# Attention plus gated MLP: later rows regrouped through DRAM and turned by VectorE, last stores split in two

## The chip, the cores and the metric

The kernel runs on one core of a Trainium2 chip. The metric is the device time of one execution in microseconds. Names used below: PE or TensorE (matmuls; its weight loads are PEld), DVE or VectorE, ACT or ScalarE, POOL or GpSimd, and SP, the engine whose queue issues most DMAs. SBUF is the on-chip memory, PSUM holds the matmul results in eight banks, DRAM is the off-chip memory.

## The reference

One layer over 2048 rows of 640 values: a layer norm, then the sum of the input, a sliding-window attention (32 heads of 20, window 256) and a gated MLP (width 1536).

```python
xn = _layernorm(x)                               # x: (1, 2048, 640), bfloat16
# A: attention
qkv = (xn @ wqkv) -> q, k, v                     # 32 heads, Dh = 20
scores = einsum("bhqd,bhkd->bhqk", q, k) * Dh ** -0.5
mask = (i - j >= 0) & (i - j < 256)
A = softmax(where(mask, scores, -1e9)) @ v -> (1, 2048, 640) @ wo
# B: gated MLP
B = (sigmoid(xn @ w_gate) * (xn @ w_up)) @ w_down
return x + A + B
```

## The kernel before

The 2048 rows are four chunks of 512 (`c`), each of four row blocks of 128 (`s`). All matmuls contract over the partitions, so the normalized rows must stand with the 640 columns on the partitions: `xnT[c]` is 128 x 5 x 512, where plane `d` holds 128 of the 640 columns. Every weight that is multiplied with it (`wqkv`, `wg`, `wu`) lies as 128 x 5 x n with the same assignment of columns to partition and plane. Before the change, partition p of plane d is column d * 128 + p.

How `xnT` comes about differs by chunk. Chunk 0 is turned by TensorE (`transpose_rows`, L276: five identity matmuls for a row block, then a copy from PSUM). Chunks 1 to 3 go through `g_norms` (L343): statistics of the four row blocks, a few steps of pause, then `norm_block` writes a normalized block `xn`, and `turn_block` (L283) has SP issue a DMA transpose of it into `xnT[c]`; for chunk 3 the transposes are issued by a generator of their own, `g_turns`.

A hand-written order runs everything. The attention scores (`scores`, L487 matmuls, L493 exponential on ScalarE, masks on GpSimd at L504) come in 76 steps; after each, the class `Fill` issues as much of the other work as fits a credit. That other work is a list of parts: "gu0a" and "gu0b" (gate and up projections of chunk 0, in halves of 5 matmuls; `pg` at L411, `pu` at L418, and the product `h` on VectorE at L422), then "x2" (load of chunk 2's rows), "wo_i" (eight DRAM-to-DRAM copies that rearrange `wo`, L212), "wd" (five loads, L205), "pads" (two clears of scratch, L178), "qk1" (q and k projections of chunk 1), "v1", "out0" (down projection, `y` at L432 and L439, and the output rows), "x3", "qk2" and so on. `mix` lets the steps of `g_norms` slip in between: after every step of "gu0b" one step of chunk 1's, after every step of "out0" one of chunk 2's, and chunk 3's in "gu1b" and in every second step of "out1". Each engine's instructions, and each queue's DMAs, run in the order in which they are issued.

What the steps below touch:

- The input rows of a chunk lie in the tile `xc`, of which there is one buffer (`pool("xp", 1)`). A new load into it (L140) waits until the last reader of the old rows is done.
- A projection (`proj_block`, L297) fills a PSUM bank, VectorE (q) or ScalarE (k) casts it into a tile `st` (L301, L303), and SP stores that to a DRAM scratch (L305). There are six `st` buffers. `spread` (L315) loads q and k back with heads on partitions.
- The PSUM pool `ps_d` has four banks and serves `pqk`, `pv`, `pg`, `pu`, `y` and the attention sum `acc` (L520) in turn; `ps`, the scores, has one buffer of four banks.
- `finish_group` and `scale_group` run on VectorE after each `acc` (L532 to L548), and `add_x` (L443) adds the input rows to `y`.
- The last row block of chunk 3 is finished in three column pieces (0 to 320, 320 to 512, 512 to 640), each stored by one DMA, on ACT's, SP's and ACT's queue.

Of the kernel before, what the change touches and what calls it, by code (L numbers as in the profile page):

```python
# [9 lines left out]
P = 128  # L10
S = 2048
D = 640
# [3 lines left out]
DC = D // P  # L16
FC = F // P
CW = 512
NCH = S // CW
SBC = CW // P  # L20
# [6 lines left out]
FS = 768  # L27
# [10 lines left out]
BF16 = mybir.dt.bfloat16  # L38
# [7 lines left out]
U = 64  # L46
# [47 lines left out]
def kernel(  # L94
# [11 lines left out]
    nc = tc.nc  # L106
    x2 = A_x.flatten_outer_dims()
    out2 = out.flatten_outer_dims()
# [26 lines left out]
    xc = {}  # L135
# [4 lines left out]
        nc.sync.dma_start(out=t, in_=xr[:, c * SBC:(c + 1) * SBC, :])  # L140

    wqkv = [const.tile([P, DC, D], BF16, name="w" + part) for part in "qkv"]
    wqkv_r = A_wqkv.rearrange("(c p) n -> p c n", p=P)
    wg = [const.tile([P, DC, FS], BF16, name=f"wg{k}") for k in range(F // FS)]
    wu = [const.tile([P, DC, FS], BF16, name=f"wu{k}") for k in range(F // FS)]
    wd = const.tile([P, FC, D], BF16, name="wd")
# [32 lines left out]

    def load_gu(t, w, k, lo=0, hi=FS):  # L180
        nc.sync.dma_start(out=t[k][:, :, lo:hi],
                          in_=w.rearrange("(c p) f -> p c f", p=P)[:, :, k * FS + lo:k * FS + hi])

    load_gu(wg, B_w_gate, 0, 0, FS // 2)
    load_gu(wu, B_w_up, 0, 0, FS // 2)
    clear("q", 0)
    clear("k", 0)
# [33 lines left out]
    ident = const.tile([P, P], BF16, name="ident")  # L221
# [24 lines left out]
    xnT = {}  # L246
    xns = {}
# [13 lines left out]
    def ln_block(c, s, mv=None):  # L261
        return ln_mv(ln_half(c, s, 1, ln_half(c, s, 0)), mv)

    def rstd_blocks(mvs):
        rstds = lnp.tile([P, SBC], FP32, name="rstds", bufs=1)
        nc.gpsimd.tensor_scalar(out=rstds, in0=mvs[:, :, 1], scalar1=EPS, scalar2=None, op0=ADD)
        nc.gpsimd.tensor_tensor(out=rstds, in0=rstds, in1=neghalf, op=POW)
        return rstds

    def norm_block(c, s, mv, rstd):  # L270
        xn = lnp.tile([P, D], BF16, name="xn")
        nc.vector.tensor_scalar(out=xn, in0=xc[c][:, s, :], scalar1=mv[:, 0:1],  # L272
                                scalar2=rstd[:, 0:1], op0=SUB, op1=MULT)
        xns[c, s] = xn

    def transpose_rows(s, copy, lo=0, hi=DC):  # L276
        pt = ps_h.tile([P, DC, P], BF16, name="pt", tag="h")
        for d in range(lo, hi):
            nc.tensor.transpose(pt[:, d, :], xns[0, s][:, d * P:(d + 1) * P], ident)  # L279
        copy(out=xnT[0][:, lo:hi, s * P:(s + 1) * P], in_=pt[:, lo:hi, :])  # L280

    def turn_block(c, s):
        nc.sync.dma_start(out=xnT[c][:, :, s * P:(s + 1) * P], in_=xns.pop((c, s)), transpose=True)  # L283

    def new_xnT(c):
        xnT[c] = xtp.tile([P, DC, CW], BF16, name="xnT")
# [53 lines left out]

    MM = 216

    def g_norms(c, turn, gap=3):  # L343


        new_xnT(c)
        mvs = lnp.tile([P, SBC, nc.vector.BN_AGGR_DIM], FP32, name="mvs", bufs=1)
        for s in range(SBC):
            ln_block(c, s, mvs[:, s, :])
            if s == SBC - 1:  # L350
                rstds = rstd_blocks(mvs)
            yield 0
        for _ in range(gap):
            yield 0
        for s in range(SBC):
            norm_block(c, s, mvs[:, s, :], rstds[:, s:s + 1])
            yield 0
            if turn:
                turn_block(c, s)

    def g_turns(c):
        for s in range(SBC):
            turn_block(c, s)
            yield 0

    def g_qk(c):
        for w in "qk":
            for m in range(DC):
                proj_block(w, c, m)
                if c == 0 and w == "q" and m == 1:  # L370
                    load_x(1)
                if c == 0 and w == "q" and m == 3:
                    load_gu(wu, B_w_up, 0, FS // 2)
                if c == 1 and w == "q" and m == 3:
                    load_wo()
# [27 lines left out]
    def part(w, d, f):  # L403
        k, first = divmod(f * P, FS)
        return w[k][:, d, first:first + P]

    def g_gu(c, f0, f1):
        for f in range(f0, f1):
            pg = ps_d.tile([P, CW], FP32, name="pg", tag="d")
            for d in range(DC):  # L410
                nc.tensor.matmul(pg, lhsT=part(wg, d, f), rhs=xnT[c][:, d, :],  # L411
                                 start=(d == 0), stop=(d == DC - 1))
            th = tp.tile([P, CW], FP32, name="th")
            nc.scalar.activation(out=th, in_=pg, func=TANH, scale=0.5)  # L414
            yield 5 * MM
            pu = ps_d.tile([P, CW], FP32, name="pu", tag="d")
            for d in range(DC):
                nc.tensor.matmul(pu, lhsT=part(wu, d, f), rhs=xnT[c][:, d, :],  # L418
                                 start=(d == 0), stop=(d == DC - 1))
            h = hp.tile([P, CW], BF16, name="h")  # L420
            ht[c, f] = h
            nc.vector.scalar_tensor_tensor(out=h, in0=th, scalar=1.0, in1=pu, op0=ADD, op1=MULT)  # L422
            yield 5 * MM
# [6 lines left out]
    def down(c, s, y, cut):  # L430
        for f in range(FC):
            nc.tensor.matmul(y[:, 0:cut[1] - cut[0]], lhsT=ht[c, f][:, s * P:(s + 1) * P],  # L432
                             rhs=wd[:, f, cut[0]:cut[1]], start=(f == 0), stop=False)
            if f % 6 == 5:
                yield 6 * 136
# [11 lines left out]
    def new_rows(c, s, name="rows", bufs=3, queue=nc.sync):  # L447
        rows = lnp.tile([P, D], BF16, name=name, bufs=bufs)
        queue.dma_start(out=rows, in_=xr[:, c * SBC + s, :])
        return rows  # L450

    def store(c, s, rows, cut=(0, D), queue=nc.sync):
        sb = c * SBC + s
        queue.dma_start(out=out2[sb * P:(sb + 1) * P, cut[0]:cut[1]], in_=rows[:, cut[0]:cut[1]])

    def outp(c, s, ys, rows):
        for y, cut in zip(ys, HALVES):
            add_wo(c, s, y, cut)
        for y, cut in zip(ys, HALVES):
            add_x(y, cut, rows)  # L460
        store(c, s, rows)

    def g_out(c, between, ahead=()):
        nxt = new_rows(c, 0)
        for s in range(SBC):
            rows = nxt
# [128 lines left out]
    def mix(a, b, first, every=1, rest=True):  # L595

        for k, cost in enumerate(a):
            yield cost
            if k >= first and (k - first) % every == 0:
                yield next(b, 0)  # L600
        if rest:
            yield from b
# [74 lines left out]
    fill = Fill()  # L677
    GU = 10 * MM
    OUT = 4 * 34 * 136
    APART = 1800  # L680
    FIRST_PART = 1000
    def later(load, *args):
        load(*args)
        yield 0

    norms1 = g_norms(1, True)
    norms2 = g_norms(2, True)
    norms3 = g_norms(3, False, 6)
    fill.add("gu0a", mix(g_gu(0, 0, 4), norms1, 4, 1, False), 4 * GU)
    fill.add("gu0b", mix(g_gu(0, 4, 12), norms1, 0), 8 * GU)  # L690
    fill.add("x2", later(load_x, 2), 0)
# [7 lines left out]
    fill.add("qk2", g_qk(2), 50 * MM)  # L699
    fill.add("v2", mix(g_v(2), g_gu(1, 3, 7), 0, 1), 40 * 136 + 4 * GU)  # L700
    fill.add("gu1b", mix(g_gu(1, 7, 12), norms3, 0, 1, False), 5 * GU)
    fill.add("out1", mix(g_out(1, g_gu(2, 0, 1)), itertools.chain(norms3, g_turns(3)), 1, 2), OUT + GU)
    fill.add("qk3", g_qk(3), 50 * MM)
    fill.add("v3", mix(g_v(3), g_gu(2, 1, 5), 0, 1), 40 * 136 + 4 * GU)
    fill.add("gu2", g_gu(2, 5, 12), 7 * GU)
# [8 lines left out]
    cuts = [(ends[n, NG - 2] + 2 + n, f"out{n}") for n in range(NCH - 1)] + [(len(todo), None)]  # L714
# [4 lines left out]
    for t, (c, k, o, step) in enumerate(todo):  # L719
# [11 lines left out]
        pt, late = scores(c, o, step)  # L731
        parts.setdefault((c, o), []).append((step, pt))
        last, label = next(x for x in cuts if t < x[0])
# [10 lines left out]
    c = NCH - 1  # L744
# [6 lines left out]
    rows = [new_rows(c, s, *home, queue=nc.scalar) for s, home in enumerate(homes)]  # L751
# [8 lines left out]
    last = SBC - 1  # L760
    cuts = (HALVES[0], (HALF, 4 * P), (4 * P, D))
# [8 lines left out]
    add_down(last, cuts[1], ps_d, "d")  # L770
    for s in range(1, last):
        outp(c, s, [ys[s, cut] for cut in HALVES], rows[s])
    for cut, queue in zip(cuts, (nc.scalar, nc.sync, nc.scalar)):
        if cut == cuts[2]:
            add_down(last, cut, ps_y, "y")
        add_wo(c, last, ys[last, cut], cut)
        add_x(ys[last, cut], cut, rows[last])
        store(c, last, rows[last], cut, queue)
# [1 line left out]
_INS = ['A_x', 'A_wqkv', 'A_wo', 'B_x', 'B_w_gate', 'B_w_up', 'B_w_down']  # L780
_OUTS = [((1, 2048, 640), 'bfloat16')]
# [25 lines left out]
```

## Time and profile before

Three runs took 308.99, 309.4 and 310.95 us; the median is 309.4 us. One execution was profiled; its page gives the span from the first to the last instruction, and what lies around it is not on the page.

| | |
|---|---|
| median of 3 runs | 309.4 us |
| span of the profiled execution | 307.5 us |
| TensorE busy | 299.6 us |
| VectorE busy | 170.7 us |
| ScalarE busy | 198.4 us |
| GpSimd busy | 169.3 us |
| DMA: SP's queue (q1), share of 16 engines | 37.3% |
| granted TensorE clock, mean | 1.000 |

The lines shown in the prediction are of three kinds. A line of the page's first part gives an engine's busy time, its share of the span and its instructions. A line of the timeline gives start, duration (both in us), engine, source line, operation, output and input tiles, and how many instructions are merged in it; a bracket at its end tells what the engine waited for. A line of a tile's answer gives shortest, median and longest duration in ns and when the first and the last started.

### The profile page before, as it was taken

What the parts mean: (1) busy time and instruction counts of PE and PEld (TensorE: products, weight loads), DVE (VectorE), ACT (ScalarE), POOL (GpSimd) and SP (SyncE); (2) the same over time, 40 slices, a digit from 0 to 9 for tenths busy, and PEclk for the clock granted to TensorE, in tenths of its full rate; (3) what the DMA queues carried; (4) which work ended last, traced back from release to release, by engine and by line L of the source; (5) the groups of instructions that cost most, each with busy time, mean ns of one, the idle gap of its engine ahead of it and who ended that gap; (6) DMA issues with size and microseconds to landing.
All of it is one profiled execution on the core that took longest, in us unless ns stands there. A gap on an engine that the chain in (4) does not pass through costs nothing.

```text
span 307.5 us, 9944 instructions
## 1 busy us (share of the span) xinstructions
PE 299.6 (97%) x4276; PEld 167.5 (54%) x4311; DVE 170.7 (56%) x339; ACT 198.4 (65%) x197; POOL 169.3 (55%) x308
## 2 busy tenths in 40 slices
PE   7999999999999999999999999999999999999995
PEld 3654444555657654554457654554546664444774
DVE  5633666639698364487946164392824536363523
ACT  6933877698855649888674547878585547687000
POOL 6000686787874828576683729467372937566000
PEclk9999999999999999999999999999999999999999
DMA  7997976986407352820002712730000200000202
GB/s 215 366 344 236 324 158 214 337 238 209 154 2 139 58 179 68 272 83 2 3 3 67 129 58 87 250 122 0 5 0 2 87 26 21 2 2 7 83 21 67
DMA packets 40460, 35.68 MB, mean 116 GB/s; under 512 B 10560, under 2 KB 39872, under 8 KB 40384
## 3 DMA queue, kind: packets, MB, share of 16 engines
q1 hardware_dynamic: 39552, 34.27, 37.3%
q10 hardware_dynamic: 864, 0.77, 0.9%
q8 instruction: 34, 0.56, 0.8%
q14 instruction: 10, 0.08, 0.1%
HBM read 23.63 MB, written 10.26 MB: 110 GB/s over the span
## 4 chain that ended last, share of the span: by engine, by line
PE 96%; issue 1%; DMA 1%; DVE 1%; ACT 0%; SPq 0%
PE y L432 18%; PE pu L418 17%; PE pg L411 17%; PE pqk L297 14%; PE ps L487 9%; PE pv L326 7%; PE y L439 7%; PE acc L520 6%; DMA xc<-in_A_x_dram 1%; PE pt L279 0%; ACT xn L617 0%; DVE xn L272 0%; DVE xn L628 0%; SPq L156 0%; DVE stats L252 0%
## 5 line engine op out<-in xcount | busy, mean ns | idle before, releaser
L504 POOL TENSOR_SCALAR_AFFINE_SELECT pT<-pT 64x512 bf16<-64x512 bf16 (+1 forms) x256 | 157.7, 616 | 108.1 <-ACT pT L493 95.6
L493 ACT ACTIVATE pT<-ps 128x2048 bf16<-128x2048 f32 (+1 forms) x76 | 141.0, 1855 | 59.6 <-PE ps L487 54.6
L422 DVE SCALAR_TENSOR_TENSOR h<-th,pu 128x512 bf16<-128x512 f32 x48 | 32.8, 684 | 52.6 <-PE pu L418 46.1
L418 PE MATMUL pu<-xnT,wu 128*128 128x512 bf16 x228 | 59.0, 380 | 0.7 <-issue 0.2
L411 PE MATMUL pg<-xnT,wg 128*128 128x512 bf16 x226 | 58.5, 380 | 0.9 <-issue 0.3
L432 PE MATMUL y<-wd,h 128*128 128x320 bf16 (+2 forms) x396 | 56.7, 295 | 0.0
L432 PEld LDWEIGHTS <-h 128*128 128x128 bf16 x396 | 36.7, 98 | 15.8 <-issue 2.0
L414 ACT ACTIVATE th<-pg 128x512 f32<-128x512 f32 x48 | 28.6, 595 | 15.5 <-PE pg L411 15.4
L411 PEld LDWEIGHTS <-wg 128*128 128x128 bf16 x240 | 22.2, 98 | 25.8 <-issue 1.8
L418 PEld LDWEIGHTS <-wu 128*128 128x128 bf16 x240 | 22.0, 98 | 25.5 <-issue 2.0
L487 PE MATMUL ps<-qT,kT 20*64 20x320 bf16 (+4 forms) x1440 | 32.1, 260 | 0.0
L532 DVE STREAM_TRANSPOSE t<-acc 128x512 f32<-128x512 f32 x32 | 21.1, 697 | 19.7 <-PE acc L520 19.7
L487 PEld LDWEIGHTS <-kT 20*64 20x64 bf16 x1440 | 15.4, 103 | 24.9 <-issue 21.8
L443 DVE SCALAR_TENSOR_TENSOR rows<-y,rows 128x320 bf16<-128x320 f32 x30 | 14.4, 488 | 25.5 <-PE y L439 25.3
L544 DVE TENSOR_TENSOR on<-t,rec 128x320 bf16<-128x320 f32 (+4 forms) x48 | 27.8, 580 | 1.1
L326 PE MATMUL pv<-wv,xnT 128*128 128x320 bf16 x160 | 25.7, 300 | 0.0
L439 PE MATMUL y<-wo,oc 128*128 128x320 bf16 (+2 forms) x165 | 24.2, 295 | 0.0
L297 PE MATMUL pqk<-xnT,wk 128*128 128x512 bf16 x97 | 23.1, 381 | 0.2
L297 PE MATMUL pqk<-xnT,wq 128*128 128x512 bf16 x94 | 22.8, 381 | 0.4 <-issue 0.2
L335 DVE CAST v<-pv 64x320 bf16<-64x320 f32 x29 | 14.1, 486 | 12.5 <-PE pv L326 12.3
L520 PE MATMUL acc<-pT,v 64*32 64x320 bf16 (+4 forms) x1440 | 19.7, 253 | 0.0
L520 PEld LDWEIGHTS <-v 64*32 64x32 bf16 x1440 | 16.2, 91 | 5.8 <-ACT pT L493 1.7
(50 smaller groups left out, 178.7 us busy)
## 6 DMA issues: line engine op xcount, KB each, us to landing
qT<-sq SPq DMA_DIRECT2D x16, 256.0 KB
kT<-sk SPq DMA_DIRECT2D x16, 256.0 KB
sq<-st SPq DMA_DIRECT2D x20, 128.0 KB
sk<-st SPq DMA_DIRECT2D x20, 128.0 KB
out_dram<-rows SPq DMA_DIRECT2D x15, 160.0 KB
wg<-in_B_w_gate_dram SPq DMA_DIRECT2D x4, 480.0 KB
wu<-in_B_w_up_dram SPq DMA_DIRECT2D x4, 480.0 KB
xc<-in_A_x_dram SPq DMA_DIRECT2D x3, 640.0 KB
```

Source lines behind the costliest of these rows:

```text
L297: nc.tensor.matmul(ps, lhsT=wt[:, m, :], rhs=xnT[c][:, d, :], start=(d == 0), stop=(d == DC - 1))
L326: nc.tensor.matmul(ps[:, 0:HALF], lhsT=xnT[c][:, d, s * P:(s + 1) * P], rhs=wqkv[2][:, d, hf * HALF:(hf + 1) * HALF], start=(d == 0), stop ...
L411: nc.tensor.matmul(pg, lhsT=part(wg, d, f), rhs=xnT[c][:, d, :], start=(d == 0), stop=(d == DC - 1))
L414: nc.scalar.activation(out=th, in_=pg, func=TANH, scale=0.5)
L418: nc.tensor.matmul(pu, lhsT=part(wu, d, f), rhs=xnT[c][:, d, :], start=(d == 0), stop=(d == DC - 1))
L422: nc.vector.scalar_tensor_tensor(out=h, in0=th, scalar=1.0, in1=pu, op0=ADD, op1=MULT)
L432: nc.tensor.matmul(y[:, 0:cut[1] - cut[0]], lhsT=ht[c, f][:, s * P:(s + 1) * P], rhs=wd[:, f, cut[0]:cut[1]], start=(f == 0), stop=False)
L439: nc.tensor.matmul(y[:, 0:cut[1] - cut[0]], lhsT=oc[c, m][:, s * P:(s + 1) * P], rhs=wo[:, m, cut[0]:cut[1]], start=False, stop=(m == DC - 1))
L487: nc.tensor.matmul(ps[a * U:(a + 1) * U, i, col * U:(col + n) * U], lhsT=qk["k", kc, o // GH][32 * i:32 * i + DH, o % GH + a, kb * U:(kb + ...
L493: nc.scalar.activation(out=pt[:, :, 0:width], in_=ps[:, :, 0:width], func=EXP, scale=SCALE)
L504: nc.gpsimd.affine_select(out=view, in_=view, pattern=[[0, HG], [0, n], [sign, U]], compare_op=GE, fill=0.0, base=base, channel_multiplier ...
L520: nc.tensor.matmul(acc[32 * i:32 * i + 32, q * U:(q + n) * U], lhsT=vt[kb][a * U:(a + 1) * U, u, h * VW:h * VW + 32], rhs=pt[a * U:(a + 1) ...
```

## The change

Three things change.

- The assignment of columns: partition p of plane d is now column p * 5 + d. The weights `wqkv`, `wg` and `wu` are loaded in that order, and chunk 0's identity transposes read every fifth column.
- Chunks 1 to 3: `turn_block` and `g_turns` go. After a block is normalized, `put_block` stores it to a DRAM scratch `xs`. When all four are stored, `regroup` loads the chunk back in four DMAs, one for each 32 partitions, into the chunk's own `xc` tile: partition 32 b + j gets, of every row with number j modulo 32, the columns 160 b to 160 b + 159. After `lag` more steps, `turn` has VectorE transpose 32 x 32 blocks, one instruction per plane, which read every fifth element of `xc` and write `xnT`. In chunk 3 these steps run in "out1", with a lag of 2.
- The last row block: each of the three column pieces is stored in two halves of 64 rows, the first from SP's queue and the second from ACT's.

```diff
-    wqkv_r = A_wqkv.rearrange("(c p) n -> p c n", p=P)
+    wqkv_r = A_wqkv.rearrange("(p c) n -> p c n", c=DC)
...
-                          in_=w.rearrange("(c p) f -> p c f", p=P)[:, :, k * FS + lo:k * FS + hi])
+                          in_=w.rearrange("(p c) f -> p c f", c=DC)[:, :, k * FS + lo:k * FS + hi])
...
-            nc.tensor.transpose(pt[:, d, :], xns[0, s][:, d * P:(d + 1) * P], ident)
+            nc.tensor.transpose(pt[:, d, :], xns[0, s].rearrange("p (i d) -> p d i", d=DC)[:, d, :], ident)
...
-    def turn_block(c, s):
-        nc.sync.dma_start(out=xnT[c][:, :, s * P:(s + 1) * P], in_=xns.pop((c, s)), transpose=True)
+    xs = [tc.dram_tile([CW, D], BF16, name=f"xs{k}") for k in range(2)]
+
+    def put_block(c, s):
+        nc.sync.dma_start(out=xs[c % 2][s * P:(s + 1) * P, :], in_=xns.pop((c, s)))
+
+    def regroup(c):
+
+        rows = xs[c % 2].rearrange("(t j) (b f) -> b j t f", j=32, b=4)
+        for b in range(4):
+            nc.sync.dma_start(out=xc[c][32 * b:32 * b + 32].rearrange("j s (a f) -> j (s a) f", a=4), in_=rows[b])
+
+    def turn(c, d):
+        nc.vector.transpose(out=xnT[c][:, d, :], in_=xc[c].rearrange("p s (t d) -> p d (s t)", d=DC)[:, d, :])
...
-    def g_norms(c, turn, gap=3):
-
-
-        new_xnT(c)
+    def g_norms(c, gap=3, lag=3):
...
             norm_block(c, s, mvs[:, s, :], rstds[:, s:s + 1])
+            put_block(c, s)
             yield 0
-            if turn:
-                turn_block(c, s)
-
-    def g_turns(c):
-        for s in range(SBC):
-            turn_block(c, s)
+        regroup(c)
+        for _ in range(lag):
+            yield 0
+        new_xnT(c)
+        for d in range(DC):
+            turn(c, d)
             yield 0
...
-    norms1 = g_norms(1, True)
-    norms2 = g_norms(2, True)
-    norms3 = g_norms(3, False, 6)
+    norms1 = g_norms(1)
+    norms2 = g_norms(2)
+    norms3 = g_norms(3, 6, 2)
...
-    fill.add("out1", mix(g_out(1, g_gu(2, 0, 1)), itertools.chain(norms3, g_turns(3)), 1, 2), OUT + GU)
+    fill.add("out1", mix(g_out(1, g_gu(2, 0, 1)), norms3, 1, 2), OUT + GU)
...
-    for cut, queue in zip(cuts, (nc.scalar, nc.sync, nc.scalar)):
+    for cut in cuts:
...
-        store(c, last, rows[last], cut, queue)
+        for half, queue in enumerate((nc.sync, nc.scalar)):
+            a, b = half * U, (half + 1) * U
+            queue.dma_start(out=out2[S - P + a:S - P + b, cut[0]:cut[1]], in_=rows[last][a:b, cut[0]:cut[1]])
```

More of the change, by code (lines that the diff above doesn't have):

```diff
@@ L450, in new_rows, with store @@
         return rows
-    def store(c, s, rows, cut=(0, D), queue=nc.sync):
+    def store(c, s, rows):
         sb = c * SBC + s
-        queue.dma_start(out=out2[sb * P:(sb + 1) * P, cut[0]:cut[1]], in_=rows[:, cut[0]:cut[1]])
+        nc.sync.dma_start(out=out2[sb * P:(sb + 1) * P, :], in_=rows)
     def outp(c, s, ys, rows):
```

## The prediction, made before the changed kernel ran

> **What bounds the kernel now.** I read the page first, then the chain that ended last, then the order of instructions on SP, VectorE, ScalarE and TensorE between 38 and 80 us, where chunk 1's rows are turned.
>
> ```profile
> span 307.5 us, 9944 instructions
> ...
> PE 299.6 (97%) x4276; PEld 167.5 (54%) x4311; DVE 170.7 (56%) x339; ACT 198.4 (65%) x197; POOL 169.3 (55%) x308
> ...
> PE 96%; issue 1%; DMA 1%; DVE 1%; ACT 0%; SPq 0%
> ```
>
> TensorE is busy for 97% of the span and makes up 96% of the chain. An edit beside it can gain only in the first 6 us and the last 4; anything that makes TensorE wait adds its full length. So the question is which queue becomes late enough to stop TensorE. The change works on SP's queue and VectorE:
>
> ```profile
> 39.32 5.27 SPq L283 DMA_TRANSPOSE xnT<-xn  x4
> 44.64 0.70 SPq L140 DMA_DIRECT2D xc<-in_A_x_dram  x1
> 45.40 5.04 SPq L212 DMA_DIRECT2D wo_i<-in_A_wo_dram  x8
> 50.48 4.34 SPq L205 DMA_DIRECT2D wd<-in_B_w_down_dram  x5
> 55.19 0.60 SPq L178 DMA_DIRECT2D sq<-kT  x1
> 56.15 0.56 SPq L178 DMA_DIRECT2D sk<-kT  x1
> 57.24 5.30 SPq L305 DMA_DIRECT2D sq<-st  x4
> 62.60 2.07 SPq L217 DMA_DIRECT2D wo<-wo_i  x4
> 64.76 0.53 SPq L305 DMA_DIRECT2D sq<-st  x1
> 65.39 4.57 SPq L305 DMA_DIRECT2D sk<-st  x5
> ```
>
> SP issues in program order: chunk 1's four transposes, the load of chunk 2's rows (x2, at 44.64), eight wo copies, five wd loads, two clears of the pads, and only then the stores of chunk 1's projections. The trace's completion records show why that order matters: the wo copies land one after another, 0.95 us apart, from 50.06 to 56.73, on only four of the DMA engines; every later transfer has a share on those four. So the first projection store, issued at 57.24, lands at 64.31, and the second at 64.66. Who needs them:
>
> ```profile
> 65.43 1.08 ACT L303 CAST st<-pqk 128x512 bf16<-128x512 f32 x2
> 66.37 1.92 ACT L493 ACTIVATE pT<-ps 128x2048 bf16<-128x2048 f32 x1
> ```
> ```profile
> 68.35 1.04 PE L520 MATMUL acc<-pT,v 64*32 64x320 bf16 x72
> 69.32 0.43 PE L487 MATMUL ps<-qT,kT 20*64 20x320 bf16 x24
> ```
>
> There are six st buffers. The two casts at 65.43 are the seventh and eighth of chunk 1, so they reuse the buffers of the first and second store. That was about 1 us to spare. Behind them on ScalarE stands an exponential; the acc matmuls at 68.35 take the two PSUM banks that these casts empty (four banks go round), and the next ps needs the exponential.
>
> **Part by part.**
>
> *Transposes out, regrouping in.* Per chunk, four DMA transposes (SP 5.27 us) go; four puts and four regroups of 160 KB come, about 8 x 0.5 = 4 us by the neighbouring issue rows, plus SP's wait for the puts. The regroup must wait until all puts have landed. Chunk 1: the last xn ends at 42.62 (VectorE's timeline), its put is issued by 43.2 and lands near 45 (1.8 us from issue to landing for a store of the same size in an idle queue, 161.66 to 163.44). Four regroup issues end near 47.3; 2048 pieces of 320 bytes at about 24 ns each (256-byte packets of the old transposes took 20 to 21) over 16 engines are 3 us, mostly under the issues; landed about 49.5, bounds 48.5 and 52.5 (pieces at 47 ns, as 1 KB packets take).
>
> *Fifteen turns on VectorE.* Nearest row: the 128x512 bf16 transpose oc<-on, 712 ns, but dense. The turn reads every fifth element; the only row with that stride is the weight load of wq and wk, 119 ns against 98 dense, 1.21 times. Bounds 0.71 and 1.42; I take 0.8. The program order puts turn 0 of chunk 1 after the ninth f's first half, turns 1 and 2 behind that f's h, turns 3 and 4 behind the next h:
>
> ```profile
> 50.31 0.29 DVE L544 TENSOR_TENSOR on<-t,rec 128x128 bf16<-128x128 f32 x1
> 50.52 0.68 DVE L422 SCALAR_TENSOR_TENSOR h<-th,pu 128x512 bf16<-128x512 f32 x1
> 51.79 0.69 DVE L422 SCALAR_TENSOR_TENSOR h<-th,pu 128x512 bf16<-128x512 f32 x1 [0.59 <-PE pu L418]
> 54.57 0.69 DVE L422 SCALAR_TENSOR_TENSOR h<-th,pu 128x512 bf16<-128x512 f32 x1 [2.09 <-ACT th L414]
> ```
>
> So the turns begin at 50.6, just after the regroup has landed (hidden by 1 us; if it lands at 52.5, 1.9 us come on top), and end at 50.6 + 5 x 0.8 + 2 x 0.6 = 55.8. VectorE was idle for 2.7 us in this stretch, so h is late by little, and four PSUM banks cover that.
>
> *The wait that the change adds.* The regroup writes into xc and the turns read it, and xc has one buffer. The load x2 therefore waits for turn 4: 55.8 instead of 44.64, 11.2 later. Queued behind it on SP are the wo copies, wd, the pads and all projection stores. What the four busy engines have to do behind x2 stays (x2 1.9, wo 7.6, wd 5.6, pads 1.9 us); without transposes ahead of x2 I give back 0.3. The first store lands at 64.31 + 10.9 = 75.2, the second at 75.5. ScalarE's two casts end near 76.4, acc starts there instead of 68.35 (+8.0); the exponential ends at 78.2, ps starts there instead of 69.32 (+8.9). The late q and k spreads catch up behind this: last store near 79, kT landed near 85, its first use 77.96 + 8.9 = 86.9. wd and wo, needed at 82.26 and 88.63 plus the same 8.9, land in time.
>
> *After the stall.* TensorE stands still for 8 us. What it does then no row of the stall can show; the nearest is the program's start:
>
> ```profile
> L232 PE MATMUL pwarm<-const-bfloat16-1.0 x10: 382/631/631, 0.8 to 4.4; 128*128 128x512 bf16 x10
> ```
>
> These ten, back to back, started 427 ns apart for 3.4 us, the later 512-column ones 216: 8 x 0.21 = 1.7 us. Bounds 0 and 3.4 (twice that); ScalarE was busy nearly throughout 72 to 78, which hides some, so I take 1.0. [...] Chunk 1: 8.9 + 1.0 = 9.9.
>
> *Chunk 2.* Last xn ends 98.15, put landed 100.2, regroup issued to 102.3, landed 104.4. Turn 0 stands ahead of add_x of row block 2 (101.36), which waits until 105.2; the next row block uses the other two banks, so this is covered until 107.4. The other four turns end near 109.5; the fifth matmul of the next projection wants the last at 108.3. Cost 0.8, bounds 0 and 3.
>
> *Chunk 3.* Two steps between turns; only the last, behind the add_x that ends at 178.6, is near its reader (179.3): 0.2, bounds 0 and 1.
>
> *Start and end.* Twenty identity transposes with strided weight loads, 20 x 21 ns at most, half covered: 0.2. The weights' new row order keeps packet count and size: 0, covered by the loads of wq and wk landing at 10.30 and 12.58 against first uses at 12.9 and 18.3; bounds 0 and 1. The last piece's two halves: 4 packets per engine instead of 8 at 18 ns, -0.07, against SP's 0.46 issue beside ScalarE's 0.35: 0, bounds -0.1 and 0.2.
>
> **Sum.** 9.9 + 0.8 + 0.2 + 0.2 + 0 = 11.1. The span of the profiled run is 307.5; the runs' median is 309.4 (308.99 to 310.95), 1.9 outside the span. Predicted span 318.6, time 320.5.
>
> **Rivals.**
>
> *Not slower* (309.6): the store chain keeps its margin. SP's part becomes shorter by about 1 us per chunk, and the queue is free of 256-byte packets. For it: the bounds of start and end, +0.2. Decides: the first store must land before about 66.5, so x2 must be issued by 47. Against: the first turn stands at 50.6 in VectorE's order. Chance 0.10.
>
> *Only the turns' own waits* (313): the buffers are not what stops TensorE, because SP packs the delayed issues closer or the stores land sooner; then remain the late regroups, chunk 1 about 1.5, chunk 2 about 1.5, others 0.6. For it: VectorE is 44% idle. Against: four engines with 17 us of work behind x2. Chance 0.17.
>
> *Dearer turns* (327): five at 1.42 move x2 by another 3.1, and chunk 2 by 2.5, start included 0.7 more. For it: the strided weight load's 1.21. Against: VectorE's transposes already take 1.4 ns an element, in float and bf16 alike (697 and 712). Chance 0.15. [...]
>
> **How the numbers follow.** The forecast has 0.58. A measurement of this kernel tells about 1% (3.1 us) from no change. Faster 0.03: a third of the first rival, through its spread, as nothing here prices a gain over 0.2. Same 0.10: the rest of it and a few of the second. Slower 0.87. The range 312 to 326 holds the forecast with its bounds and most of the second rival, and leaves out the first and half of the third.
>
> **What would show it.** Right: x2 issued near 56 instead of 44.64; no TensorE work from about 68 to 76; ScalarE's L303 waiting for a DMA there; granted clock below 1.0 in that slice; turns of 0.7 to 0.9 us; about 0.8 us lost around 108. Wrong: x2 before 50, casts of chunk 1 on time, or turns above 1.2 us.

## The result, and the profile after

The changed kernel takes 323.58 us (median of 4 runs, 322.99 to 325.89) against 309.37 us before (4 runs beside it, 308.99 to 310.95). The ratio is 1.047, with a 95% interval of 1.043 to 1.051: slower, as forecast. The forecast was 320.5 us, in a range of 312 to 326. The profiled run of the changed kernel took 323.65 us; its span grew from 307.5 to 321.9 us, 14.4 us against 11.1 in the sum.

The page of the changed kernel, the same parts as before:

```profile
span 321.9 us, 10014 instructions
...
PE 306.7 (95%) x4311; PEld 169.0 (52%) x4311; DVE 180.2 (56%) x354; ACT 198.5 (62%) x197; POOL 169.0 (52%) x308
...
PEclk9999999995999997999999999999999999999999
...
PE 83%; DMA 8%; DVE 4%; SPq 3%; issue 1%; ACT 0%; ACTq 0%; DVEq 0%
```

Before, TensorE made up 96% of the chain that ended last; now DMA, VectorE and SP's queue hold 15% of it. The granted clock (the row PEclk) has two dips, in the slice around 76 us and in the one around 125 us. TensorE's matmuls were the same (4311 weight loads both times; 35 matmul records are missing from the trace of before), so the 7 us by which its busy time grew are not more work. Matmuls at half clock (1.2 us in one group and 1.7 in another, below) and matmuls that wait one by one are part of it.

SP's queue in chunk 1 (start, length, line, operation), and from the list of waits SP's wait in front of the load x2 (total, times, longest):

```profile
40.01 3.65 SPq L285 DMA_DIRECT2D xs<-xn  x4
45.13 2.34 SPq L291 DMA_DIRECT2D xc<-xs  x4
55.91 0.40 SPq L140 DMA_DIRECT2D xc<-in_A_x_dram  x1
56.34 5.42 SPq L212 DMA_DIRECT2D wo_i<-in_A_wo_dram  x8
61.82 4.41 SPq L205 DMA_DIRECT2D wd<-in_B_w_down_dram  x5
...
68.43 3.84 SPq L316 DMA_DIRECT2D sq<-st  x4
```
```profile
SPq L140 <- DVE xnT L294: 4.6, 1, 4.6
```

x2 leaves at 55.91 instead of 44.64, and the thing that released it was a turn on VectorE (xnT, L294). Everything behind x2 is later by the same: the first projection store is issued at 68.43 instead of 57.24. A transfer counts as landed with the last of its 16 completion records: the first store landed at 75.59 (64.55 before), the second at 75.94 (64.89 before). The turns themselves, on VectorE:

```profile
51.34 0.76 DVE L294 STREAM_TRANSPOSE xnT<-xc 128x512 bf16<-128x512 bf16 x1
...
52.60 1.38 DVE L294 STREAM_TRANSPOSE xnT<-xc 128x512 bf16<-128x512 bf16 x2
...
54.48 1.40 DVE L294 STREAM_TRANSPOSE xnT<-xc 128x512 bf16<-128x512 bf16 x2
```

Who waited for the late stores: first ScalarE, then TensorE, with the cause in brackets:

```profile
75.69 1.07 ACT L314 CAST st<-pqk 128x512 bf16<-128x512 f32 x2 [9.46 <-DMA sq<-st]
```
```profile
66.76 2.35 PE L308 MATMUL pqk<-xnT,wk 128*128 128x512 bf16 x10
76.33 2.27 PE L529 MATMUL acc<-pT,v 64*32 64x320 bf16 x72 [7.22 <-ACT st L314]
78.60 0.65 PE L496 MATMUL ps<-qT,kT 20*64 20x320 bf16 x24
```

The two casts that had 1 us to spare before now wait 9.46 us for the buffer of the first store, and TensorE has nothing to do from 69.1 to 76.3. When it starts again, the same 72 acc matmuls take 2.27 us instead of 1.04. Busy time by stretches of 3 us (after the length: PE, PEld, DVE, ACT, POOL, each with its instructions, then the granted clock, DMA share, GB/s) shows the clock at half there:

```profile
67.00:70.00 3.00, 2.11 (x10) 0.94 (x8) 0.00 (x0) 0.00 (x0) 1.58 (x3) 1.00 0.99 351
70.00:73.00 3.00, 0.00 (x0) 0.00 (x0) 0.00 (x0) 0.00 (x0) 0.00 (x0) 1.00 0.92 348
73.00:76.00 3.00, 0.00 (x0) 0.00 (x0) 0.00 (x0) 0.31 (x1) 0.00 (x0) 0.53 0.84 262
76.00:79.00 3.00, 2.64 (x96) 1.82 (x96) 0.56 (x1) 3.00 (x5) 0.39 (x1) 0.50 0.87 258
```

From 69.1 to 75.7 no compute engine runs, while the DMA engines are busy at a mean of 0.90. The clock record is at 0.5 from 73.21 to 80.04. The slow acc matmuls themselves cost next to nothing, though: they end at 78.60, and the exponential on ScalarE that the next ps needs anyway ended at 78.55 (76.65 + 1.90, behind the two casts).

**Where the 14.4 us are.** The program has 76 groups of score matmuls (ps). Their starts, after minus before, rise only at a few places, and this gives the loss stage by stage:

| stage | forecast | measured | from |
|---|---|---|---|
| start | 0.2 | 0.69 | all groups to 67 us are later by 0.69 |
| chunk 1 | 9.9 | 9.21 | +0.69 becomes +9.28 at the ps of 78.60, +9.90 at the next |
| chunk 2 | 0.8 | 3.62 | +9.80 becomes +11.73, then +13.42 |
| chunk 3 | 0.2 | 0.07 | +13.41 becomes +13.48 |
| end | 0 | 0.92 | 14.4 less 13.48 |

(0.1 us came back between chunks 1 and 2.) Chunk 2's two steps, on TensorE and on VectorE:

```profile
117.18 0.38 PE L308 MATMUL pqk<-xnT,wq 128*128 128x512 bf16 x1
118.07 0.38 PE L308 MATMUL pqk<-xnT,wq 128*128 128x512 bf16 x1 [0.51 <-DVE xnT L294]
...
119.98 0.38 PE L308 MATMUL pqk<-xnT,wq 128*128 128x512 bf16 x1 [0.26 <-DVE xnT L294]
120.28 0.42 PE L496 MATMUL ps<-qT,kT 20*64 20x256 bf16 x16
120.64 5.12 PE L308 MATMUL pqk<-xnT,wq 128*128 128x512 bf16 x15
```
```profile
115.83 0.76 DVE L294 STREAM_TRANSPOSE xnT<-xc 128x512 bf16<-128x512 bf16 x1 [4.82 <-DMA xc<-xs]
116.51 0.85 DVE L452 SCALAR_TENSOR_TENSOR rows<-y,rows 128x320 bf16<-128x320 f32 x2
117.28 2.64 DVE L294 STREAM_TRANSPOSE xnT<-xc 128x512 bf16<-128x512 bf16 x4
```

VectorE waited 4.82 us for the regroup, so the five matmuls of the first projection went at the pace of the turns, one every 0.64 us instead of every 0.21: 1.93 us. The 15 behind them then took 5.12 us instead of 3.43, at half clock: 1.69 us more.

An experiment below issues the regroup earlier and tests whether both steps go with it.

At the start and at the end, TensorE's wait for the second half of wv, and the six issues of the last pieces on SP and on ScalarE's queue:

```profile
9.14 2.21 PE L337 MATMUL pv<-wv,xnT 128*128 128x320 bf16 x15 [0.51 <-DMA wv<-in_A_wqkv_dram]
```
```profile
316.61 2.21 SPq L789 DMA_DIRECT2D out_dram<-xn  x3
```
```profile
316.62 2.48 ACTq L789 DMA_DIRECT2D out_dram<-xn  x3
```

### The profile page after: what moved, and what is told of

Its sections match the earlier page's. It is cut to its first block, busy times and chain, and to the rows that moved or that the text cites. A ratio compares the mean times of both kernels' runs of the same rounds, so it can differ in the third digit from the quotient of the medians.

```text
span 321.9 us, 10014 instructions
## 1 busy us (share of the span) xinstructions
PE 306.7 (95%) x4311; PEld 169.0 (52%) x4311; DVE 180.2 (56%) x354; ACT 198.5 (62%) x197; POOL 169.0 (52%) x308
## 4 chain that ended last, share of the span: by engine, by line
PE 83%; DMA 8%; DVE 4%; SPq 3%; issue 1%; ACT 0%; ACTq 0%; DVEq 0%
PE pu L427 16%; PE pg L420 16%; PE y L441 15%; PE pqk L308 11%; PE ps L496 7%; PE pv L337 7%; PE y L448 6%; PE acc L529 6%; DMA sq<-st 2%; DMA wo_i<-in_A_wo_dram 2%; DMA wv<-in_A_wqkv_dram 2%; DVE xnT L294 2%; DMA xc<-xs 1%; SPq L212 1%; DMA xs<-xn 1%
## 5 line engine op out<-in xcount | busy, mean ns | idle before, releaser
L427 PE MATMUL pu<-xnT,wu 128*128 128x512 bf16 x240 | 59.8, 380 | 0.0
L420 PE MATMUL pg<-xnT,wg 128*128 128x512 bf16 x240 | 59.8, 380 | 0.0
L529 PE MATMUL acc<-pT,v 64*32 64x320 bf16 (+4 forms) x1440 | 20.9, 259 | 7.3 <-ACT st L314 7.2
L308 PE MATMUL pqk<-xnT,wq 128*128 128x512 bf16 x100 | 25.7, 401 | 1.3 <-DVE xnT L294 1.3
L314 ACT CAST st<-pqk 128x512 bf16<-128x512 f32 x20 | 11.2, 602 | 16.8 <-DMA sq<-st 9.5
```

What stands on the lines that cost most here:

```text
L308: nc.tensor.matmul(ps, lhsT=wt[:, m, :], rhs=xnT[c][:, d, :], start=(d == 0), stop=(d == DC - 1))
L529: nc.tensor.matmul(acc[32 * i:32 * i + 32, q * U:(q + n) * U], lhsT=vt[kb][a * U:(a + 1) * U, u, h * VW:h * VW + 32], rhs=pt[a * U:(a + 1) ...
```

## The experiments

The theory: the regroup uses xc, xc has one buffer, so x2 waits for the turns; SP's order carries that wait to the projection stores, the st buffers carry it to ScalarE, and the four PSUM banks to TensorE. The rivals: TensorE is stopped by the added work itself (eight more SP issues, 320-byte pieces, turns), or the fixed cost is in the work queued behind x2, or most of the loss is the clock. The losses by stage below are taken from the starts of the score groups against the kernel before, as in the table. Where no number of runs is given, there was one. Runs of the changed kernel lie 2.9 us apart, so a single time that differs by less than that says little, and the stages of the profiled run carry the argument.

**Take x2's wait away.** The regrouped rows land in the four xn tiles, made one tile of the same size. The puts have read them by then, so no load has to wait for a turn. (The same tile also serves chunk 0's and the very last rows, which the excerpt below leaves out.)

```
 def norm_block(c, s, mv, rstd):
-    xn = lnp.tile([P, D], BF16, name="xn")
+    xn = new_xn(c, s)          # xn4[c][:, s, :], xn4 = [P, SBC, D], one buffer
...
-    nc.sync.dma_start(out=xc[c][32 * b:32 * b + 32].rearrange(...), in_=rows[b])
+    nc.sync.dma_start(out=xn4[c][32 * b:32 * b + 32].rearrange(...), in_=rows[b])
...
-    nc.vector.transpose(out=xnT[c][:, d, :], in_=xc[c].rearrange(...)[:, d, :])
+    nc.vector.transpose(out=xnT[c][:, d, :], in_=xn4[c].rearrange(...)[:, d, :])
```

> The changed kernel, with one thing taken away: the regrouped rows land in the four xn tiles (made one tile of the same size), which the puts have already read, and no longer in xc. So x2 has no turn to wait for. If the wait on xc's only buffer is what stops TensorE in chunk 1: x2 is issued right behind the regroup at about 48 instead of 55.9, the first projection store lands at about 68 instead of 75.4, the casts come some 1 to 2 us late, and chunk 1 loses 1 to 3 us instead of 9.2; with start 0.7, chunk 2 3.0 and end 0.9 as in the changed kernel this gives about 316 us (314 to 318.5). Rival (the eight SP issues, the 320-byte pieces and the turns themselves delay the stores, not the buffer): chunk 1 still loses more than 5 us and the time stays above 319.

Measured: 315.41 us (4 runs, 313.78 to 319.02), ratio to before 1.018 (1.015 to 1.021). SP's queue, ScalarE's two casts and the clock row of the profiled run (315.37 us, span 313.6):

```profile
45.56 3.08 SPq L298 DMA_DIRECT2D xn<-xs  x4
48.67 0.49 SPq L140 DMA_DIRECT2D xc<-in_A_x_dram  x1
49.21 5.31 SPq L212 DMA_DIRECT2D wo_i<-in_A_wo_dram  x8
...
61.34 3.84 SPq L323 DMA_DIRECT2D sq<-st  x4
```
```profile
68.49 1.07 ACT L321 CAST st<-pqk 128x512 bf16<-128x512 f32 x2 [1.64 <-DMA sq<-st]
```
```profile
PEclk9999999999999999999999999999999999999999
```

x2 goes right behind the regroup, the first store lands at 68.39, the casts wait 1.64 us for it instead of 9.46, and the clock never falls. Chunk 1 loses 2.0 us instead of 9.2: 1.16 because qk1 now waits for turns, 0.87 because of the casts. The regroup, the eight issues and all 15 turns are still there, so they are not the stall; the buffer is. Of the 8.3 us between the two spans, 7.2 are in chunk 1; chunk 2 brings 1.2 (2.43 instead of 3.62, with no fall of the clock) and the start 0.5, and the end takes back 0.6.

**Move x2 in the order instead.** x2 keeps its wait, but stands behind the pads, so that wo and wd no longer wait with it.

```
-    fill.add("x2", later(load_x, 2), 0)
     fill.add("wo_i", later(turn_wo), 0)
     fill.add("wd", later(load_wd), 0)
     fill.add("pads", later(clear_next), 0)
+    fill.add("x2", later(load_x, 2), 0)
```

> The load of chunk 2's rows is issued behind the wo copies, the wd loads and the pads instead of ahead of them. Theory (that load waits for the last turn of chunk 1, everything behind it on SP is late, and the late projection stores keep the st buffers from ScalarE): the copies start near 48 instead of 56.3, the first store of chunk 1 lands near 68 instead of 75.4, TensorE's wait of 7.2 us before acc falls under 1, the clock drop there goes too; of the 9.2 us lost in chunk 1 at most 1.5 stay: 314 to 316 us. Rival (the turns and the regroup hold up TensorE, whatever SP does behind them): no change, 323.6 us.

Measured: 320.67 us, span 319.0. Chunk 1 lost 5.3 instead of 9.2, so the direction is right, but the size is not: I had expected 314 to 316. x2 is a transfer on all 16 engines, landed at 71.64, and the first store, issued behind it, at 71.93. So the store was still late, now behind the transfer of x2 and not behind its wait; that this is the whole of the 5.3 us is not shown by this run, but with x2 behind the stores as well (the first of the versions put together, below) chunk 1 lost 1.7. About 1.5 us more than expected came from the start, where this run lost 2.14, with a wait for wv (0.39 us) and a record of low clock at 7.31 to 10.72.

**More st buffers.** Nine instead of six.

```
-    stp = pool("stp", 6)
+    stp = pool("stp", 9)
```

> Nine st buffers instead of six; SP's order as in the changed kernel. Theory: the wait moves from the seventh cast of chunk 1 to the tenth, which must still wait for the first store (landed near 75.4) and holds back the exponential behind it; TensorE stands for some 5 us instead of 7.2, now at the matmuls behind acc, with the clock drop as before: about 320.5 us, and k's reload comes just in time. Rival A (the buffers are not what stops TensorE, but the late reload of k for chunk 1's scores): 323.6 us, TensorE waiting for kT. Rival B (with three buffers more nothing waits): 314 to 315 us.

Measured: 323.27 us, span 321.2, a miss. The wait moved by one group and became shorter, as expected; the whole did not follow. TensorE and ScalarE of this kernel:

```profile
69.02 1.04 PE L529 MATMUL acc<-pT,v 64*32 64x320 bf16 x72
...
77.98 0.55 PE L496 MATMUL ps<-qT,kT 20*64 20x320 bf16 x16 [5.02 <-ACT pT L502]
```
```profile
75.56 0.58 ACT L314 CAST st<-pqk 128x512 bf16<-128x512 f32 x1 [6.12 <-DMA sq<-st]
```

acc is on time and the tenth cast waits for the first store (landed 75.46) instead of the seventh. Chunk 1's loss fell from 9.2 to 7.1, but chunk 2's was 5.3 us instead of 3.6; why it grew is not shown. Buffers postpone the wait; they do not bring the store earlier.

**Spread the wo copies over 16 engines.** They ran on four DMA engines; here each is cut into pieces of 1600 bytes.

```
-   nc.sync.dma_start(out=wo_i[i].rearrange("(b a d) n -> a b d n", ...)[a],
-                     in_=A_wo.rearrange("(a b i d) n -> i a b d n", ...)[i, a])
+   nc.sync.dma_start(out=wo_i[i].rearrange("(b a d) n -> a b (d n)", ...)[a].rearrange("b (x e) -> x b e", x=16),
+                     in_=A_wo.rearrange("(a b i d) n -> i a b (d n)", ...)[i, a].rearrange("b (x e) -> x b e", x=16))
```

> The eight wo copies are written as 64 pieces of 1600 bytes over 16 DMA engines instead of 4 pieces of 25,600 bytes on four. Theory (the store lands late since four engines hold 7.6 us of copies ahead of it): the first store lands near 69 to 70.5 instead of 75.4, acc waits 1 to 2.5 us instead of 7.2, hardly a clock drop: 316 to 318.5 us. Rival (SP's own issues are the limit, the copies are covered): first store near 74, 322 us or more.

Measured: 322.35 us, span 320.6; a miss, and as the rival had it (first store near 74, 322 us or more), though not for the rival's reason. The copies landed by 64.85 instead of 68.36, but wd then landed to 71.8, the pads at 73.98, the first store at 74.16 instead of 75.59. acc waited 6.20 us. The low clock stretched over 70.71 to 80.95 and chunk 1 lost 9.4 all the same. So the four engines were not the only limit behind x2. Nor were SP's issues: the first store was issued at 66.89 and landed 7.3 us later, with the DMA engines fully busy from 68 to 75 (share 1.02 and more). What was left ahead of it was the data of x2, wd and the pads.

**Keep TensorE busy through the stall.** The last k projection of chunk 1 gets 30 more matmuls. The added loop does not set wt again, so all 30 multiply the weights of the last plane, and what stays is another product than before, against the expectation's "the same result". The matmuls are of the same size; only the times of this kernel are of use.

```
+        for d in range(6 * DC if (w, c, m) == ("k", 1, DC - 1) else 0):
+            d %= DC
+            nc.tensor.matmul(ps, lhsT=wt[:, m, :], rhs=xnT[c][:, d, :],
+                             start=(d == 0), stop=(d == DC - 1))
```

> TensorE repeats the last k projection of chunk 1 six times (30 more matmuls, the same result), so that it works for 6.5 us of the 7.2 that it stood. Theory (after the stall it runs at half its clock, because it stood): acc starts at the same time, near 76.3, but its 72 matmuls take about 1.05 us instead of 2.27, the granted clock stays at 1.0 there, and the scores that follow come 1.3 to 1.9 us sooner: about 322 us. Rival (the slow matmuls after the stall have another cause, such as waits on ScalarE, or ScalarE sets the pace there anyway): 323.6 us.

TensorE's matmuls in this kernel:

```profile
68.99 6.64 PE L312 MATMUL pqk<-xnT,wk 128*128 128x512 bf16 x29
76.98 0.32 PE L533 MATMUL acc<-pT,v 64*32 64x320 bf16 x4 [1.36 <-ACT st L318]
77.47 1.00 PE L533 MATMUL acc<-pT,v 64*32 64x320 bf16 x68 [0.17 <-ACT st L318]
79.25 0.65 PE L500 MATMUL ps<-qT,kT 20*64 20x320 bf16 x24 [0.78 <-ACT pT L506]
```

The clock stayed up through the stall (1.00 from 76 to 79), and the 72 acc matmuls took 1.32 us instead of 2.27: that they were slow because TensorE had stood still is shown. But nothing was gained. The next ps still waited 0.78 us, for the exponential (pT), which sets its start whatever the clock. And the waits of 1.36, 0.17 and 0.78 left TensorE busy for 1.36 us of the 3.41 from 75.88 to 79.29, and the record shows 0.5 from 79.29 to 82.71 directly behind. Chunk 1 lost 10.8. The time, 326.52 us (span 324.8), holds besides a single pause of 2.3 us near 217 us which no other run here has, and whose cause stays open.

**Chunk 2's norms two steps earlier.**

```
-    norms2 = g_norms(2)
+    norms2 = g_norms(2, 1)
```

> Chunk 2's rows are normalized two steps earlier (a pause of one step instead of three); all else as in the changed kernel. Theory (the regroup takes 5.7 us from its first issue to its landing, the first turn stands ready 4.8 us before, and TensorE then waits for turn after turn until its clock is halved for one window): the regroup lands near 112.6 instead of 115.8, all five turns are done before the next projection wants them at 117.2 to 118, neither the wait of 1.9 us nor the 1.7 us of half clock is left: 3.6 us less, 320 us (319.5 to 320.5). Rival (VectorE has too much to do there, not too late data): 323 us or more.

TensorE at the same place of the program as above:

```profile
118.34 0.81 PE L308 MATMUL pqk<-xnT,wq 128*128 128x512 bf16 x2
119.33 0.38 PE L308 MATMUL pqk<-xnT,wq 128*128 128x512 bf16 x1 [0.17 <-DVE xnT L294]
...
120.26 0.42 PE L496 MATMUL ps<-qT,kT 20*64 20x256 bf16 x16
120.62 3.43 PE L308 MATMUL pqk<-xnT,wq 128*128 128x512 bf16 x15
```

Chunk 2's loss fell from 3.62 to 0.75 us, and the 15 matmuls take 3.43 us, as before the change. So chunk 2's loss is the late regroup, and the low clock behind it is its consequence. The whole time nevertheless stayed at 323.52 us in this one run: its low clock in chunk 1 lasted 10.24 us (71.94 to 82.18), the start lost 1.16, and the end 1.4 more than in the changed kernel, with a last landing 3.7 us after its issue. All three lie far from the edited place. As a whole time it is inconclusive; the stage is clear.

**The parts at both ends, alone, in the kernel before.** First the split stores of the last rows:

```
-    for cut, queue in zip(cuts, (nc.scalar, nc.sync, nc.scalar)):
+    for cut in cuts:
...
-        store(c, last, rows[last], cut, queue)
+        for half, queue in enumerate((nc.sync, nc.scalar)):
+            a, b = half * U, (half + 1) * U
+            queue.dma_start(out=out2[S - P + a:S - P + b, cut[0]:cut[1]], in_=rows[last][a:b, cut[0]:cut[1]])
```

> The kernel before with the last row block's three pieces stored in halves from two queues, nothing else. Theory (issues on both queues at once take 0.54 to 0.98 us each instead of 0.33 to 0.46, and the last waits for the one before it): the time from the last add_x to the end of the span grows by 0.9 us: 310.3 us. Rival (the longer end of the changed kernel belongs to its other parts): no difference, 309.4 us.

Measured: 310.00 us (10 runs, 309.76 to 311.78) against 309.15 (25 runs, 308.95 to 311.82), ratio 1.002 (0.9996 to 1.0043). The interval cannot tell it from no change, but the profile shows 0.6 us at the end: all score groups start as before, the last add_x ends at 304.26 in both, and the span ends at 308.1 instead of 307.5. Three of the six stores, those on SP's queue:

```profile
303.12 2.35 SPq L780 DMA_DIRECT2D out_dram<-xn  x3
```

Then the weights' row order alone. This kernel pairs the weights' rows with other columns of x, so only its times are of use.

```
-    wqkv_r = A_wqkv.rearrange("(c p) n -> p c n", p=P)
+    wqkv_r = A_wqkv.rearrange("(p c) n -> p c n", c=DC)
...
-        in_=w.rearrange("(c p) f -> p c f", p=P)[:, :, k * FS + lo:k * FS + hi])
+        in_=w.rearrange("(p c) f -> p c f", c=DC)[:, :, k * FS + lo:k * FS + hi])
```

> The kernel before with the three weights loaded in the new order of columns, nothing else (the rows keep the old order, so another product of the same size is computed). Theory (the start is later because the second half of wv lands about 1 us later in this order): the first scores come 0.3 to 0.7 us later, 309.7 to 310.1 us, in some runs 1.5 us more if the clock falls for a window there. Rival (the start is later because chunk 0's identity transposes read every fifth column): no difference, 309.4 us.

Measured: 310.12 us (10 runs, 308.97 to 311.19), ratio 1.0016 (0.9988 to 1.0044), so as a time not to be told from no change. Four of the runs lie at 310.9 to 311.2 and the rest at 309 to 310.4; of the 25 runs of the kernel before, three lie at 310.9 to 311.8. In the profiled one (311.19) all scores start 1.93 us later than before: the halves of wv landed at 6.65 and 9.88 (6.54 and 8.07 before), and the clock reached 1.0 only at 10.06. In that run the order cost 1.9 us, with wv late and the clock late; whether the slower ones of the other nine have the same cause is not shown.

**Versions put together.** All three take the earlier norms and the whole stores. The first keeps the regroup in xc and moves x2 behind the value projections ("v1"):

```
-    norms2 = g_norms(2)
+    norms2 = g_norms(2, 1)
...
-    fill.add("x2", later(load_x, 2), 0)
...
     fill.add("v1", ...)
+    fill.add("x2", later(load_x, 2), 0)
...
-        for half, queue in enumerate((nc.sync, nc.scalar)):
...
+        store(c, last, rows[last], cut, queue)
```

> The changed kernel with its three waits taken away: the load of chunk 2's rows is issued behind chunk 1's projections and values (after v1), chunk 2 is normalized two steps earlier, and the last pieces are stored whole as before. Theory (the time was lost in SP's order, the late regroup of chunk 2 and the split stores; the regrouping itself is hidden): only the start's 0.3 to 0.7 us and at most 0.5 us in chunk 1 stay: 310.2 us (309.7 to 311.0), no gain over the kernel before, since TensorE was at work 97% of its span. Rival (regrouping and turns cost TensorE time of their own): 313 us or more.

Measured: 311.87 us (11 runs, 310.65 to 315.12), ratio 1.0066 (1.004 to 1.0091): above the expected range by 0.9, and 1.1 under the rival's 313. The profiled run is the slowest of the eleven (315.12, span 313.3): start 0.6, chunk 1 1.7, chunk 2 1.8, end 1.5. So neither side was right: the stall is gone, but regroup and turns still cost TensorE some time. The second has the regroup in xn's tile, and the next rows' load ahead of the regroup:

```
+        if c < NCH - 1:
+            load_x(c + 1)
         regroup(c)
```

> The kernel with the regroup in its own buffer, and besides: the loads of the next chunk's rows stand ahead of the regroup on SP, chunk 2's norms start two steps earlier (gap 1), and the last pieces are stored whole as before. x2 is issued near 44, the wo copies from 47.5, the first projection store lands near 67: chunk 1 loses 0 to 1.5 us, chunk 2 under 1, start 0.7, end 0. About 311.3 us (310.3 to 313). If a stall of several us comes back, something other than the buffer holds the stores; faster than the kernel before, 309.4, only if the order around the start and the queue gains, which nothing measured so far speaks for.

Measured: 313.71 us (4 runs, 312.85 to 315.08), ratio 1.013 (1.011 to 1.016), a miss. In the profiled run (315.08, span 313.4) the casts lose nothing and the end nothing, but qk1 waited 1.3 us for its turns and chunk 2 lost 3.9. Its regroup was issued from 100.42, against 103.18 without the earlier norms, but x3's 640 KB lay ahead of it (landed 104.79), it landed at 108.22, and the clock fell once more (a mean of 0.69 from 112 to 115 and 0.74 from 115 to 118). The third therefore keeps the loads away from the regroups: x2 behind "v1" again, x3 where it was.

```
-        if c < NCH - 1:
-            load_x(c + 1)
         regroup(c)
...
     fill.add("v1", ...)
+    fill.add("x2", later(load_x, 2), 0)
     fill.add("out0", ...)
+    fill.add("x3", later(load_x, 3), 0)
```

> The regroup in xn's tile, the earlier norms of chunk 2 and the whole stores, with no load of rows near a regroup on SP: x2 stands behind the value projections, x3 where it was. In the version with the loads ahead of the regroup, chunk 2's regroup was issued early (100.4) and landed late (107.75), because 640 KB of rows lay ahead of it. Without them it should land about 4 us behind its first issue, at 104 to 105, and chunk 1's by 50: no waits for turns in chunk 1 (1.3 there) and under 1 us in chunk 2 (3.9 there), casts late by 0 to 1. With start 0.5 and end 0: about 310.6 us (309.8 to 312). If the regroup still lands past 107 or the time stays above 312.5, the way through DRAM is slow by itself and not for the load ahead of it. Faster than before by over 1 us: nothing measured speaks for it.

Measured: 311.56 us (6 runs, 311.09 to 313.05), ratio 1.0076 (1.005 to 1.0105), within the range. The profiled run (313.04, one of the two slowest) has span 311.2 and clock 1.00: start 0.05, chunk 1 0.7, with no wait for a turn, chunk 2 1.7, end 1.2. In chunk 2 the regroup was issued from 100.20, and VectorE still waited for it:

```profile
106.48 2.04 DVE L301 STREAM_TRANSPOSE xnT<-xn 128x512 bf16<-128x512 bf16 x3 [5.82 <-DMA xn<-xs]
```

That is 6.3 us from the first issue to the first turn with no load ahead of it, where I had expected a landing about 4 us behind the issue. The end's 1.2 us was not expected either: the last store, whole as before, took 3.0 us from its issue to its landing (306.79 to 309.78), against 1.8 in the kernel before. The first version's profiled run shows the same (3.25 us), the second's does not (1.7). Why it varies is open, so a late end is not always the split's. None of the three reaches the kernel before. Of the changed kernel's 14 us the queue order, the buffer, the earlier norms and the stores together account for nearly 12 (311.56 against 309.0 leaves 2.6); in the last version's trace the largest part of the rest is the way through DRAM in chunk 2, then the end.

## Why the prediction was right, and which terms were off

The mechanism of chunk 1 held at every link: x2 at 55.91 (forecast 55.8), the first store at 75.59 (75.2) and the second at 75.94 (75.5), the casts waiting for a DMA, no TensorE work from 69 to 76, a granted clock of 0.5 behind it, turns of 0.71 to 0.77 us (0.8). (The prediction took each landing one completion record early where a transfer on four engines had used the same semaphore: 64.31 and 64.66 are 64.55 and 64.89, and the copies' 50.06 to 56.73 are 50.11 to 57.09.) Its 9.9 us were 9.2. The sum had 8.0 for the stall, 0.9 for the exponential behind it and 1.0 for the clock, an estimate from the ten matmuls at the start of the kernel before, in whose trace no fall of the clock behind a stall was to be seen. Measured: acc started at 76.33 as forecast (76.4), but 0.69 of that had been lost at the start, which leaves 7.3; the exponential ended at 78.55 and put ps 1.3 further behind; and the half clock, recorded from 73.21 to 80.04, added 0.6 up to the next ps. Errors of less than 1 us that partly cancel.

That x2's time came out to 0.1 us is partly luck. The start was late by 0.69, the turns were shorter than 0.8 us, and the regroup landed at 51.22, not 49.5, which is within its bounds but only 0.06 us ahead of the moment when VectorE was free (51.28).

*Dearer turns* is ruled out by the durations: the 15 turns with their ten-byte steps took 0.71 to 0.77 us, median 0.73, against 0.71 for the dense transpose oc<-on. So VectorE's transpose at this step took 0.02 us more in the median, where the rival had 1.42 us a turn. *Only the turns' own waits* is what remains when the buffer is taken away: 315.4 us were measured there, against its 313. *Not slower* fell with x2's wait.

The sum was 3.3 us short, and chunk 1 had 0.7 too much. The three terms below make up that difference. Two of them lie outside their own bounds; the time stayed within the range because the other terms' bounds and the rivals had made it wide.

- *Chunk 2*, 0.8 forecast with a bound of 3, measured 3.62. Two things failed. The regroup's landing: four issues from 110.06, landed at 113.04, 114.07, 114.86 and 115.81. That is about 0.92 us apart for 512 pieces each, 32 per engine, 29 ns a piece where I took 24 (the packet records of these pieces have the same mean). And I had counted the pieces as lying under the issues, and no time behind the last one: the last packet of data ended at 114.73, its completion came 1.1 us later. First issue to last landing was 5.75 us instead of some 4.2. And the clock: I counted half rate only for the long stall, and 3.41 us of it (121.00 to 124.41) came here too. The earlier norms, which took the wait away, brought 2.9 us of the 3.6 back.
- *End*, 0 with a bound of 0.2, measured 0.92. I costed the transfer and left out the issues: six from two queues at once took 0.54 to 0.98 us each, where before three had taken 0.35 to 0.46, and the last two were issued at 318.22 and 318.28 for an add_x that ended at 317.74; the longer of them ended at 319.10. The split stores alone gained nothing and ended 0.6 us later (308.1 against 307.5).
- *Start*, 0.2 with the weights' new order at 0, measured 0.69. I had looked at wq and wk for cover and not at wv, whose second half TensorE waits for: landed at 9.10 instead of 8.07, wait 0.51. Its issues took 0.70 and 0.57 us instead of 0.43, though bytes and packets are the same.

## What to carry to other kernels

Ask of each new use of a buffer who was the next to write it, and follow that writer's queue to its end: here a VectorE transpose of 0.7 us held a load, and behind the load a whole queue of transfers that had nothing to do with it. Reusing a buffer whose readers were already waited for removed the stall without any change of the work. And a wait on TensorE should be priced with the half clock that may follow it (here 6.83 us of it in chunk 1 and 3.41 in chunk 2), and a late arrival from its last completion, not from its issues (here 115.81 for four issues from 110.06).

## What the runs showed of the hardware

The clock records of the kernel before and of the changed one, but for the last of each, which begins behind the program's end, are whole multiples of one length, 3.413 us. In the changed kernel's trace those at 0.5 are 6.83 us (73.21 to 80.04) and 3.41 us long (121.00 to 124.41), two and one of them; those at 1.0 are 68.27, 40.96 and 197.97 us long, 20, 12 and 58. The first record begins at 4.94. The one record at 1.0 of the kernel before has 303.79 us, 89 of them, from 4.24. In the experiments, 79.29 to 82.71 (the added matmuls) is one of them and 71.94 to 82.18 (the earlier norms) three. So a stall's price in half clock went up by 3.41 us at a time in these runs. Below, a window is a stretch of that length between the records' borders. Busy time and clock of the changed kernel, in windows up to the fall in chunk 2:

```profile
114.17:117.59 3.42, 3.39 (x37) 2.04 (x36) 1.76 (x4) 1.66 (x2) 2.54 (x5) 1.00 0.07 9
117.59:121.00 3.41, 2.15 (x22) 0.77 (x22) 3.41 (x7) 0.46 (x2) 2.24 (x4) 1.00 0.15 53
121.00:124.41 3.41, 3.41 (x10) 1.22 (x9) 1.32 (x3) 1.66 (x1) 0.00 (x0) 0.50 0.45 124
```

In the window ahead of the fall TensorE was busy for 2.15 of 3.41 us, with no wait over 0.51. The kernel with the regroup in xn's tile had much the same row of waits, 0.19, 0.67 and three of 0.26, and no fall: its clock stayed at 1.00 from 106 to 118, with TensorE busy for 1.76 of the 3 us from 109 to 112. Why the one fell and the other did not is not shown.

Laid over the traces of the kernel before and of the changed one, up to the programs' ends, the windows give a rough measure. The clock fell behind those with 0 (69.80 to 73.21) and 2.15 us (117.59 to 121.00) of TensorE work, stayed at 0.5 behind one with 0.29 (73.21 to 76.62), came back behind two at half clock with 3.38 and 3.41 (76.62 to 80.04, 121.00 to 124.41), and fell behind none with 2.23 or more. With the matmuls added it fell behind one with 1.36 (75.88 to 79.29). But at the end of the changed kernel it did not fall behind one with 1.86 (315.56 to 318.97). So the work in one window alone does not settle it.

The other surprise was that issues have a price of their own: 0.33 to 0.46 us for a whole store of the last rows, 0.54 to 0.98 for the halves of 64 rows with SP and ScalarE issuing together (0.48 to 0.93 in the kernel before with the halves alone). Whether the neighbour or the shape of the halves makes the difference is not separated by any run.
